# Attention into two mixture-of-experts layers: loads, halves of mixed tiles and the logits of layer 1's last block put elsewhere

## The chip, the cores and the metric

The kernel runs on one core of a Trainium2 chip. The metric is device time in microseconds of one launch; lower is better. Engines: TensorE (PE; PEld is its weight load), VectorE (DVE), ScalarE (ACT), GpSimd (POOL), and SyncE (SP), which only issues loads and stores. Every engine executes its own instructions strictly in the order of the program, so a wait at one instruction holds everything behind it on that engine.

## The reference

```python
# attention: 8 batches, 8 heads, 576 queries, head_dim 64; k and v averaged over runs of 8 rows
k_p = k.reshape(B, H, Sp, pool, D).mean(axis=3)
v_p = v.reshape(B, H, Sp, pool, D).mean(axis=3)
scores = scale * np.matmul(q, k_p.transpose(0, 1, 3, 2))
attn = softmax(scores);  x = attn @ v_p          # 4608 tokens of 512
# layer 1: 8 experts, top 1
logits = x @ w_gate + modality_bias[modality_id]
e_idx = np.argmax(logits, axis=1)
x = gate_w[:, None] * (relu(x @ w1[e_idx]) @ w2[e_idx])
# layer 2: the same with a skip score, and the input added
do_compute = x @ w_skip > 0
out = x.copy()
out[do_compute] += gate_w * (relu(x @ w1[e]) @ w2[e])     # experts by argmax(x @ w_gate)
```

## The kernel before, in words

**Attention.** The 4608 query rows are 36 columns of 128, nine for each pair of batches. A unit of q is a half-batch of 256 rows (two columns, one load of 512 KB into `q_sb`); the last 64 rows of both batches of a pair make up a merged column (numbers 8, 17, 26, 35), whose halves belong to different batches (`parts(c)`). Keys and values come in as raw tiles (`kb` or `kt`, and `v`), are summed over runs of 8 rows by VectorE (line 176) or GpSimd (lines 181 to 183), turned by TensorE (`prep_kb`, line 203 on) and stand as `KB` and `VB`. For column c, ScalarE spreads q (`split_q`, line 167), TensorE turns it (line 280), ScalarE copies it (`qt`, line 284), `emit_S` (line 296) makes scores against `KB`, VectorE takes the maximum `mx` (line 307), TensorE subtracts it (line 327), ScalarE takes exp (331), TensorE turns the result (348), and `emit_AV` (line 355) multiplies by `VB`. `emit_S` and `emit_AV` loop over `parts(c)` outside and over head pairs inside, so a merged column has all instructions of its first half, then all of its second. Each fp32 matmul appears twice in the trace: 8 and 12 instructions in a regular column, 16 and 24 in a merged one.

The order around the loads is written by hand: the prologue (lines 482 to 495) issues the first loads on SyncE's queue, and `wg`, `midi`, `bb` (router weights, modality ids, bias) on ScalarE's; the loop over c (line 560 on) issues q with `next_q`, keys and values with `next_kv`; `pool_at` (line 424) says at which c which sums are taken; VectorE's work of a column is put behind the `mx` of the next. 24 transposes of the identity keep TensorE at work while the first load is on its way (lines 512 to 514).

**Layer 1** works in blocks of 256 sorted tokens (halves t = 0, 1): gathered rows are turned into `xh` and `xl`, `gemm1` (line 1402) has 8 steps f, each followed by `hh` (ACT, 1406) and `hl` (DVE, 1407); `gemm2` (line 1455) has 8 steps per half. The blocks' outputs are layer 2's inputs: for each half 9 sums on VectorE (8 logits and the skip score, line 1734, `logit`) are queued in `todo` together with `first` and `second`, the two parts of layer 2's routing of that block (`picks`, lines 1660 to 1722: chains of small GpSimd and VectorE steps that end in the scatter of the rows). `drip(n)` takes steps of cost n off that queue, at the f's that `body1` (line 1895) sets by hand. Blocks 0 to 17 always run; 17 is `late`: it also loads what follows. Behind it a dynamic `If` runs further blocks where the routing needs them; with this input the trace has one more, 18 (`end` is set in its body). Behind that `first2` (line 1593) makes layer 2's first block: its `gemm1` steps alternate with what is left of block 18's logits, and `late_logits` (line 1576) makes the second half's 9 on TensorE instead: 4 transposes, a copy, 4 small matmuls. Then come `first` (f = 2), `second` and the last gather of layer 2's input (f = 4), whose rows the first `gemm2` turns.

Of the kernel before, what the change touches and what calls it, by code (L numbers as in the profile page):

```python
# [9 lines left out]
F32 = mybir.dt.float32  # L10
# [45 lines left out]
def attention(tc, g, q, k, v, mid, w_gate, bias, const, moe):  # L56
# [4 lines left out]
    with ExitStack() as ctx:  # L61
# [140 lines left out]

        def prep_kb(b, eng=None):
# [5 lines left out]
            for i in range(4):  # L209
                nc.tensor.transpose(ps[0:64, 126 * i:126 * i + 126], ks[0:126, i, :],  # L210
                                    g.ident[0:126, 0:126])
                nc.tensor.matmul(ps[64:128, 126 * i:126 * i + 126], lhsT=ks[0:126, i, :],
                                 rhs=g.ident[0:126, 0:126], start=True, stop=True)

            nc.tensor.matmul(ps[64:128, 0:SP], lhsT=ks[0:SP, 4, :], rhs=g.ident[0:SP, 0:SP],
                             start=True, stop=True)
            view = lambda c: ps[:, c:c + 6 * SP].rearrange("p (a s) -> p a s", s=2 * SP)[:, :, 0:SP]
# [78 lines left out]
        def emit_S(c, then=lambda: None):  # L296
            t = qT.pop(c)
            ps = ps_s.tile([128, 2, 512], F32, tag="s", name="ps_s")
            for b, p0, p1 in parts(c):
                for hp in range(4):  # L300
# [56 lines left out]
        def emit_AV(c):  # L357
# [7 lines left out]
            for b, p0, p1 in parts(c):  # L365
                for j in range(6):
                    o = (j % 3) * VW
# [49 lines left out]
        def idle():  # L417
            for _ in range(3):
# [5 lines left out]
        pool_at = {0: [(pool_kb, 1, 2, 4, P)],  # L424
                   1: [(pool_kb, 1, 0, 2, V), (pool_kb, 1, 4, 5, V), (pool_v, 1, 0, P)]}
# [64 lines left out]
        for i in range(2):  # L490
            nc.scalar.dma_start(out=wg[64 * i:64 * i + 64],
                                in_=w_gate.rearrange("(h d) e -> d h e", d=64))
        nc.scalar.dma_start(out=midi,
                            in_=mid.bitcast(I32).rearrange("(b s w) -> b s w", s=S, w=2))
        nc.scalar.dma_start(out=bb, in_=bias.unsqueeze(0).to_broadcast([128, 2, E]))
# [14 lines left out]
        P.memset(WGV, 0.0)  # L510

        ps = ps_q.tile([128, 4, 128], F32, tag="q", name="ps_w")
        for i in range(24):
            nc.tensor.transpose(ps[:, i % 4, :], g.ident, g.ident)
# [44 lines left out]
        for c in range(NC + LAG):  # L559
            if c < NC:  # L560
                next_q(cols[c][0] + 4)
                next_kv(c)
                next_q(cols[c][0] + 5)
# [607 lines left out]
class Moe:  # L1171
# [404 lines left out]
    def late_logits(self, i):  # L1576

        nc = self.nc
        ps = self.ps_t("ps_x2")
        for k in range(4):  # L1580
            nc.tensor.transpose(ps[:, k, :], self.x2[i % 2][:, 1, 128 * k:128 * k + 128],
                                self.g.ident)
        xt = self.o2[1].rearrange("p (k n) -> p k n", k=4)
        nc.scalar.copy(xt, ps)
        yield
        lg = self.pp.tile([128, E + 1], F32, tag="m", name="ps_lg")
        for k in range(4):
            nc.tensor.matmul(lg, lhsT=xt[:, k, :], rhs=self.g.w9c[:, k, :], start=(k == 0),
                             stop=(k == 3))
        nc.vector.tensor_copy(self.lg2[i % 2][:, 1, :], lg)  # L1590
        yield

    def first2(self, n):
# [4 lines left out]
        todo = [x for x in self.todo[:-11]]  # L1598
# [4 lines left out]
        for f in range(8):  # L1603
            self.gemm1(n, f)
            for x in todo[2 * f:2 * f + 2 if f < 7 else None]:
                x[2]()
            if f in (0, 2):
                next(late)
# [150 lines left out]
class Layer:  # L1759
# [129 lines left out]
    def body1(self, i, end):  # L1889
# [35 lines left out]
        if more:  # L1925
            m.load_split(i + 1)
            if end is None:
                m.gates1(i + 1, m.sp)
            m.split_w1_if(range(4))
        at = {f: m.drip for f in ((0, 1, 3, 5) if late else (0, 1, 5, 6) if i > 8 else  # L1930
                                  (0, 1, 3, 5, 6))}
# [3 lines left out]
        if more and late:  # L1935
            m.drip(3)
            next_x(0)
            next_x(1)
            m.split_w1_if(range(4, 8))
            m.drip(4)  # L1940
        else:
            if more:
                m.split_w1_if(range(4, 8))
            m.drip(7)
        with m.tc.If(full > 0):
# [127 lines left out]
```

## Time and profile before

| what | value |
|---|---|
| median of 3 runs | 964.8 us (963.85 to 965.71) |
| the profiled execution's own time | 967.72 us |
| its span in the trace | 966.0 us |
| mean granted clock of TensorE in it | 0.966 |
| attention alone on TensorE, and mixed with layer 1's first blocks | to about 78 us, and to about 230 us |
| layer 1's block 17, `gemm2` | 643.8 to 656.8 us |
| block 18 | 658.0 to 682.6 us |
| layer 2's first block: `gemm1`, and its first `gemm2` | 682.5 to 700.3, and to 719.9 us |

A row of the timeline gives the start, the duration of a run of like instructions, the engine and line, what it writes and reads with shapes, and in brackets the idle time before it with what released it. The granted clock is a share of 2.4 GHz; 0.5 is the lower of its two levels, 1.2 GHz. Durations of TensorE overlap, since matmuls are pipelined.

### The profile page before, as it was taken

The numbers are of one execution on the slowest core, as the hardware profiler recorded it, in microseconds if no ns is written. First come the engines' busy times: TensorE is split into PE (matmuls) and PEld (weight loads), VectorE is DVE, ScalarE is ACT, GpSimd is POOL, SyncE is SP. The second block draws the span as 40 slices with busy tenths as digits, with TensorE's granted clock in tenths as the row PEclk, the third lists the DMA queues.
The fourth block names the chain that finished last, engine by engine and source line by source line (L and its number), as shares of the span: only waits on it lengthen the run. The fifth ranks groups of instructions, "written<-read, shape, count | busy, mean of one in ns | idle before, by whom it ended". The sixth has DMA issues, their size and how long they took to land. (4 is left out here: it accounts for less than half of the span.)

```text
span 966.0 us, 19093 instructions
## 1 busy us (share of the span) xinstructions
PE 908.6 (94%) x6205; PEld 813.6 (84%) x6205; DVE 696.9 (72%) x1844; ACT 373.2 (39%) x734; POOL 517.6 (54%) x762
## 2 busy tenths in 40 slices
PE   6899999899999999998999989999889999999995
PEld 5798898887899999996999878988868988978983
DVE  4376787765787878889877798877775667667555
ACT  2465566544122222242222332212413556565454
POOL 4744698304246547666656556575653344354443
PEclk7799999998999999998999999999999999999998
DMA  9997884521321211251223512127213774581341
GB/s 224 216 257 212 231 232 148 156 102 53 119 71 57 79 60 64 92 200 64 74 78 100 205 54 86 65 68 241 77 45 129 219 218 148 177 259 35 110 155 41
DMA packets 87225, 126.03 MB, mean 130 GB/s; under 512 B 14328, under 2 KB 51192, under 8 KB 86954
## 3 DMA queue, kind: packets, MB, share of 16 engines
q1 hardware_dynamic: 75386, 96.68, 32.9%
q0 software_dynamic: 10480, 27.59, 9.3%
q8 instruction: 62, 1.02, 0.4%
q14 instruction: 81, 0.66, 0.2%
q10 hardware_dynamic: 1216, 0.08, 0.1%
HBM read 184.18 MB, written 39.50 MB: 232 GB/s over the span
## 5 line engine op out<-in xcount | busy, mean ns | idle before, releaser
L1402 PE MATMUL ps_g<-xh,w1h 128*128 128x256 f32 x896 | 256.8, 287 | 5.7 <-DVE hl L1407 3.1
L1402 PE MATMUL ps_g<-xl,w1h 128*128 128x256 f32 x896 | 254.1, 284 | 2.6 <-DVE xl L1354 2.6
L1402 PE MATMUL ps_g<-xh,w1l 128*128 128x256 f32 x896 | 253.7, 283 | 0.0
L1734 DVE CUSTOM_DVE_ANT_0 junk<-x,W 128x512 bf16<-128x512 f32 x333 | 234.8, 705 | 19.6 <-DVEq L1332 6.6
L1455 PE MATMUL ps_g<-w2h,hh 128*128 128x512 f32 x464 | 192.9, 416 | 0.7 <-DVE rs_v L1043 0.5
L1455 PE MATMUL ps_g<-w2h,hl 128*128 128x512 f32 x464 | 186.7, 402 | 6.6 <-DVE hl L1407 6.6
L1455 PE MATMUL ps_g<-w2l,hh 128*128 128x512 f32 x464 | 186.3, 402 | 0.0
L1402 PEld LDWEIGHTS ps_g<-xh,w1h 128*128 128x128 f32 x896 | 170.6, 190 | 12.0 <-DVE hl L1407 3.5
L1402 PEld LDWEIGHTS ps_g<-xl,w1h 128*128 128x128 f32 x896 | 169.9, 190 | 4.5 <-DVE xl L1354 3.6
L1402 PEld LDWEIGHTS ps_g<-xh,w1l 128*128 128x128 f32 x896 | 169.9, 190 | 0.0
L1406 ACT ACTIVATE hh<-ps_g 128x512 fp32r<-128x512 f32 (+1 forms) x116 | 67.7, 584 | 250.8 <-PE ps_g L1402 235.2
L906 POOL TENSOR_SCALAR OB<-iota,BB,pay 128x128 bf16<-128x128 bf16 x126 | 112.2, 898 | 22.7 <-DVE BB L894 20.3
L1407 DVE SCALAR_TENSOR_TENSOR hl<-ps_g,hh 128x512 fp32r<-128x512 f32 (+1 forms) x116 | 77.5, 668 | 61.5 <-ACT hh L1406 37.7
L1455 PEld LDWEIGHTS ps_g<-w2h,hl 128*128 128x128 f32 x464 | 89.1, 192 | 30.8 <-DVE hl L1407 8.2
L1455 PEld LDWEIGHTS ps_g<-w2h,hh 128*128 128x128 f32 x464 | 89.3, 192 | 19.8 <-ACT hh L1424 1.5
L1455 PEld LDWEIGHTS ps_g<-w2l,hh 128*128 128x128 f32 x464 | 89.4, 193 | 16.9
L1322 POOL TENSOR_TENSOR w1l<-w1r,w1h 128x512 fp32r<-128x512 f32 x39 | 50.6, 1316 | 64.4 <-ACT w1h L1321 64.2
L1344 DVE TENSOR_TENSOR w2l<-w2r,w2h 128x512 fp32r<-128x512 f32 x112 | 75.2, 708 | 7.9 <-ACT w2h L1343 5.4
L1700 POOL DMA_INDIRECT out_dram<-x,dsi x38 | 46.7, 1228 | 46.7 <-ACTq L1337 10.6
L1321 ACT CAST w1h<-w1r 128x512 fp32r<-128x512 f32 x120 | 68.3, 620 | 0.5 <-ACT hh L1406 0.5
L1343 ACT CAST w2h<-w2r 128x512 fp32r<-128x512 f32 x112 | 63.9, 616 | 4.0 <-DVE gidxf L1046 2.5
L368 PE MATMUL ps_av<-VB,et 96*128 96x146 f32 (+1 forms) x480 | 64.5, 288 | 0.0
(292 smaller groups left out, 1384.7 us busy)
## 6 DMA issues: line engine op xcount, KB each, us to landing
w1r<-in_moe_w_dram SPq DMA_DIRECT2D x128, 512.0 KB
w2r<-in_moe_w_dram SPq DMA_DIRECT2D x128, 512.0 KB
x2s<-x SPq DMA_DIRECT2D x19, 522.0 KB
v<-in_v_dram SPq DMA_DIRECT2D x48, 192.0 KB
xd<-x SPq DMA_DIRECT2D x16, 520.0 KB
q_sb<-in_q_dram SPq DMA_DIRECT2D x16, 512.0 KB
kt<-in_k_dram SPq DMA_DIRECT2D x32, 144.0 KB
x2s<-OBx SPq DMA_DIRECT2D x16, 261.0 KB
```

Of the source, the lines that this page charges most:

```text
L368: nc.tensor.matmul(ps[p0:p1, j // 3, o:o + 2 * VW], lhsT=t[:, j, p0:p1], rhs=VB[b % NR][:, j].rearrange("p i w -> p (i w)"), start=(j % 3 ...
L906: e.tensor_scalar(g.ob(c)[:, i, :], g.iota, r.BB[:, c:c + 1], r.pay[:, i, c:c + 1], ALU.is_equal, ALU.mult)
L1321: self.nc.scalar.copy(self.w1h[f], raw)
L1322: (eng or self.nc.vector).tensor_tensor(self.w1l[f], raw, self.w1h[f].bitcast(F32), ALU.subtract)
L1343: self.nc.scalar.copy(self.w2h[f], raw)
L1344: (eng or self.nc.vector).tensor_tensor(self.w2l[f], raw, self.w2h[f].bitcast(F32), ALU.subtract)
L1402: nc.tensor.matmul(out, lhsT=a[f][:, k, :], rhs=b[:, k, :], start=(n == 0), stop=(n == 11))
L1406: nc.scalar.activation(out=hh, in_=whole, func=ACTF.Relu)
L1407: nc.vector.scalar_tensor_tensor(hl, in0=whole, scalar=0.0, in1=hh.bitcast(F32), op0=ALU.max, op1=ALU.subtract)
L1455: nc.tensor.matmul(ps, lhsT=a[f][:, tt], rhs=b[f], start=(n == 0), stop=(n == 23))
L1700: self.nc.gpsimd.indirect_dma_start(out=self.out, out_offset=bass.IndirectOffsetOnAxis(ap=self.dsi[i % 2][:, t:t + 1], axis=0), in_=self.x ...
L1734: self.nc.vector.tensor_tensor_reduce(out=self.junk, in0=self.x2[i % 2][:, t, 0:DM], in1=self.W9[:, e, :], scale=1.0, scalar=0.0, op0=ALU. ...
```

## The change

It has five parts. (1) At the start, `midi`, `bb` and the two `wg` loads go from ScalarE's queue to GpSimd's, behind its last memset; 12 more transposes of the identity stand in the middle of the first `prep_kb` and 10 behind it. (2) The two VectorE sums of batch 1's keys go from c = 1 to c = 0; at c = 2 the load of half-batch 5 is put ahead of that step's v load. (3) `emit_S` and `emit_AV` take the halves of a merged column in turn. (4) In block 17, `second` of block 16 is taken out of the queue, three sums are taken and both halves of block 18's rows are turned ahead of it; in the dynamic blocks behind, the queue is drained evenly from f = 0 to 7, and the last half-block's 9 sums (t = 0) are left to the block behind. (5) `first2` makes both halves' 9 logits on TensorE (f = 0, 1, 2) and has no sums on VectorE.

```diff
             d = sums_of(("v", b), [VC, 6, D])
             pool_rows(d[:, 3 * hf + i0:3 * hf + i1, :], raw_t["v", b, hf][:, i0:i1, :], eng)
 
+        def keep_busy(n):
+            ps = ps_q.tile([128, 4, 128], F32, tag="q", name="ps_w")
+            for i in range(n):
+                nc.tensor.transpose(ps[:, i % 4, :], g.ident, g.ident)
+
         def prep_kb(b, eng=None):
 
             bg.settle()
...
             ps = ps_m.tile([128, 512], F32, tag="m", name="ps_k")
             KBb = KB[b % NR]
             for i in range(4):
+                if b == 0 and i == 2:
+                    keep_busy(12)
                 nc.tensor.transpose(ps[0:64, 126 * i:126 * i + 126], ks[0:126, i, :],
                                     g.ident[0:126, 0:126])
                 nc.tensor.matmul(ps[64:128, 126 * i:126 * i + 126], lhsT=ks[0:126, i, :],
...
 
             nc.tensor.matmul(ps[64:128, 0:SP], lhsT=ks[0:SP, 4, :], rhs=g.ident[0:SP, 0:SP],
                              start=True, stop=True)
+            if b == 0:
+                keep_busy(10)
             view = lambda c: ps[:, c:c + 6 * SP].rearrange("p (a s) -> p a s", s=2 * SP)[:, :, 0:SP]
             copy = nc.vector.tensor_copy if eng is nc.vector else nc.scalar.copy
             copy(KBb[0:64, 0:3, 0:SP], view(0)[0:64])
...
         def emit_S(c, then=lambda: None):
             t = qT.pop(c)
             ps = ps_s.tile([128, 2, 512], F32, tag="s", name="ps_s")
-            for b, p0, p1 in parts(c):
-                for hp in range(4):
+            for hp in range(4):
+                for b, p0, p1 in parts(c):
                     nc.tensor.matmul(ps[p0:p1, hp // 2, (hp % 2) * 144:(hp % 2) * 144 + 144],
                                      lhsT=t[:, hp, p0:p1], rhs=KB[b % NR][:, hp, :],
                                      start=(hp % 2 == 0), stop=(hp % 2 == 1),
...
                 ps = ps_e.tile([128, 2, 512], F32, tag="et", name="ps_av")
             else:
                 ps = ps_a.tile([128, 2, 512], F32, tag="av", name="ps_av")
-            for b, p0, p1 in parts(c):
-                for j in range(6):
-                    o = (j % 3) * VW
+            for j in range(6):
+                o = (j % 3) * VW
+                for b, p0, p1 in parts(c):
                     nc.tensor.matmul(ps[p0:p1, j // 3, o:o + 2 * VW],
                                      lhsT=t[:, j, p0:p1],
                                      rhs=VB[b % NR][:, j].rearrange("p i w -> p (i w)"),
...
         av_t = {}
 
         P, V = nc.gpsimd, nc.vector
-        pool_at = {0: [(pool_kb, 1, 2, 4, P)],
-                   1: [(pool_kb, 1, 0, 2, V), (pool_kb, 1, 4, 5, V), (pool_v, 1, 0, P)]}
+        pool_at = {0: [(pool_kb, 1, 2, 4, P), (pool_kb, 1, 0, 2, V), (pool_kb, 1, 4, 5, V)],
+                   1: [(pool_v, 1, 0, P)]}
         for t, c0 in enumerate((3, 8, 16, 23)):
             pool_at[c0] = [(pool_k, t, 0, P)]
             pool_at[c0 + 1] = [(pool_k, t, 1, P)]
...
         next_kv(0, 5)
         next_q(3)
         next_kv(0, 1)
-        for i in range(2):
-            nc.scalar.dma_start(out=wg[64 * i:64 * i + 64],
-                                in_=w_gate.rearrange("(h d) e -> d h e", d=64))
-        nc.scalar.dma_start(out=midi,
-                            in_=mid.bitcast(I32).rearrange("(b s w) -> b s w", s=S, w=2))
-        nc.scalar.dma_start(out=bb, in_=bias.unsqueeze(0).to_broadcast([128, 2, E]))
 
         for i in range(NR):
             me = nc.vector if i < 1 else nc.gpsimd
...
         for i in range(NR):
             P.tensor_copy(VB[i][:, :, :, D], half)
         P.memset(WGV, 0.0)
-
-        ps = ps_q.tile([128, 4, 128], F32, tag="q", name="ps_w")
-        for i in range(24):
-            nc.tensor.transpose(ps[:, i % 4, :], g.ident, g.ident)
+        P.dma_start(out=midi, in_=mid.bitcast(I32).rearrange("(b s w) -> b s w", s=S, w=2))
+        P.dma_start(out=bb, in_=bias.unsqueeze(0).to_broadcast([128, 2, E]))
+        for i in range(2):
+            P.dma_start(out=wg[64 * i:64 * i + 64],
+                        in_=w_gate.rearrange("(h d) e -> d h e", d=64))
+
+        keep_busy(24)
 
         midf = one.tile([128, C1], F32, name="midf")
         mid8 = xp.tile([128, 2, XW], F32, tag="x", name="mid8")
...
         route_at = {12: (0, 9), 21: (9, 9), 30: (18, 9)}
         for c in range(NC + LAG):
             if c < NC:
-                next_q(cols[c][0] + 4)
+                next_q(cols[c][0] + (5 if c == 2 else 4))
                 next_kv(c)
                 next_q(cols[c][0] + 5)
             if c in (22, 32, 36):
...
     def late_logits(self, i):
 
         nc = self.nc
-        ps = self.ps_t("ps_x2")
-        for k in range(4):
-            nc.tensor.transpose(ps[:, k, :], self.x2[i % 2][:, 1, 128 * k:128 * k + 128],
-                                self.g.ident)
-        xt = self.o2[1].rearrange("p (k n) -> p k n", k=4)
-        nc.scalar.copy(xt, ps)
-        yield
-        lg = self.pp.tile([128, E + 1], F32, tag="m", name="ps_lg")
-        for k in range(4):
-            nc.tensor.matmul(lg, lhsT=xt[:, k, :], rhs=self.g.w9c[:, k, :], start=(k == 0),
-                             stop=(k == 3))
-        nc.vector.tensor_copy(self.lg2[i % 2][:, 1, :], lg)
+        xt = [o.rearrange("p (k n) -> p k n", k=4) for o in self.o2]
+        for t in range(2):
+            ps = self.ps_t("ps_x2")
+            for k in range(4):
+                nc.tensor.transpose(ps[:, k, :], self.x2[i % 2][:, t, 128 * k:128 * k + 128],
+                                    self.g.ident)
+            nc.scalar.copy(xt[t], ps)
+            yield
+        lg = self.pp.tile([128, 2, E + 1], F32, tag="m", name="ps_lg")
+        for t in range(2):
+            for k in range(4):
+                nc.tensor.matmul(lg[:, t, :], lhsT=xt[t][:, k, :], rhs=self.g.w9c[:, k, :],
+                                 start=(k == 0), stop=(k == 3))
+        nc.vector.tensor_copy(self.lg2[i % 2], lg)
         yield
 
     def first2(self, n):
...
         nc, g = self.nc, self.g
         ranks = self.ranks
         self.ranks = []
-        todo = [x for x in self.todo[:-11]]
+        for _, cost, f in self.todo[:-2]:
+            if not cost:
+                f()
         first, second, third = self.picks(n - 1, False)
         self.todo = []
         nc.vector.tensor_copy(self.gate0, self.gate[n % 2])
         late = self.late_logits(n - 1)
         for f in range(8):
             self.gemm1(n, f)
-            for x in todo[2 * f:2 * f + 2 if f < 7 else None]:
-                x[2]()
-            if f in (0, 2):
+            if f < 3:
                 next(late)
             if f == 1 and n % 2:
                 nc.scalar.copy(self.xg[0], self.xg[1])
...
             if end is None:
                 m.gates1(i + 1, m.sp)
             m.split_w1_if(range(4))
-        at = {f: m.drip for f in ((0, 1, 3, 5) if late else (0, 1, 5, 6) if i > 8 else
-                                  (0, 1, 3, 5, 6))}
+        if end is None:
+            at = {f: m.drip for f in ((0, 1, 5, 6) if i > 8 else (0, 1, 3, 5, 6))}
+        elif late:
+            at = {f: m.drip for f in (0, 1, 3, 5)}
+        else:
+            n = sum(x[1] for x in m.todo) - 2
+            at = {f: partial(m.drip, (n + j) // 5) for j, f in enumerate((0, 1, 3, 5, 6))}
+            at[7] = m.drip
         if more and not late:
             at.update({2: lambda: next_x(0), 4: lambda: next_x(1)})
         m.gemm2(i, 0, self.epilogue, at)
-        if more and late:
+        if late:
+            _, _, second = m.todo.pop(0)
             m.drip(3)
             next_x(0)
             next_x(1)
+            second()
+        if more:
             m.split_w1_if(range(4, 8))
-            m.drip(4)
-        else:
-            if more:
-                m.split_w1_if(range(4, 8))
+        if end is None:
             m.drip(7)
+        elif not late:
+            m.drip()
         with m.tc.If(full > 0):
             m.gemm2(i, 1, self.epilogue)
 
```

## Rows read from the trace of the kernel before

**Rows 1.** The page: busy time, share of the span and instructions of each engine.
```profile
PE 908.6 (94%) x6205; PEld 813.6 (84%) x6205; DVE 696.9 (72%) x1844; ACT 373.2 (39%) x734; POOL 517.6 (54%) x762
```

**Rows 2.** Stretches: busy us (instructions) of PE, PEld, DVE, ACT, POOL; granted clock; DMA share; GB/s.
```profile
0.00:20.00 20.00, 11.48 (x49) 9.17 (x50) 6.36 (x9) 4.15 (x6) 6.14 (x24) 0.75 0.90 221
20.00:44.00 24.00, 19.81 (x100) 16.18 (x100) 10.20 (x9) 10.32 (x27) 18.06 (x17) 0.64 0.99 217
44.00:78.00 34.00, 32.06 (x270) 31.05 (x270) 25.41 (x58) 21.76 (x48) 19.82 (x37) 1.00 0.91 237
```

**Rows 3.** Timeline, 0 to 22: start, duration, engine, line, operation, [idle before <- releaser].
```profile
13.10 0.57 ACTq L493 DMA_DIRECT2D midi<-in_moe_modality_id_dram  x1
...
15.92 0.62 ACT L167 COPY qs<-q_sb 128x512 f32<-128x512 f32 x1 [13.62 <-DMA v<-in_v_dram]
...
18.38 2.29 PE L301 MATMUL ps_s<-KB,qt 128*128 128x144 f32 x8 [0.68 <-ACT qt L284]
```

**Rows 4.** Timeline, 28 to 60: batch 1's keys turned, and the fourth column's scores.
```profile
34.28 0.39 PE L210 MATMUL ps_k<-ident,kb 126*64 126x126 f32 x1 [2.48 <-DVE kb L176]
...
40.38 2.27 PE L301 MATMUL ps_s<-KB,qt 128*128 128x144 f32 x8
```

**Rows 5.** Timeline, TensorE 100 to 112 and 204 to 214: scores and values, regular and merged.
```profile
101.89 1.15 PE L301 MATMUL ps_s<-KB,qt 128*128 128x144 f32 x8
...
106.01 1.74 PE L301 MATMUL ps_s<-KB,qt 128*64 128x144 f32 x16
...
110.03 0.51 PE L327 MATMUL ps_s<-mx,nident 128*128 128x288 f32 x2 [1.04 <-DVE mx L307]
...
206.54 1.66 PE L368 MATMUL ps_av<-VB,et 96*128 96x146 f32 x12
...
210.68 2.77 PE L368 MATMUL ps_av<-VB,et 96*64 96x146 f32 x24
```

**Rows 6.** Timeline, 42 to 63: loads of half-batches 5 and 6, and the copy of 6.
```profile
42.83 0.39 SPq L141 DMA_DIRECT2D q_sb<-in_q_dram  x1
...
55.59 0.39 SPq L141 DMA_DIRECT2D q_sb<-in_q_dram  x1
...
62.45 1.05 ACT L167 COPY qs<-q_sb 128x1024 f32<-128x1024 f32 x1
```

**Rows 7.** Timeline, 650 to 662: the seam between blocks 17 and 18 of layer 1.
```profile
654.88 0.17 DVE L1681 TENSOR_REDUCE rt_my<-rt_eq 128x2 f32<-128x16 f32 x1 [4.79 <-POOL rt_eq L1675]
...
656.91 0.20 POOL L1686 TENSOR_TENSOR carry<-carry,M 128x8 f32<-128x8 f32 x1
...
657.99 0.39 PE L1402 MATMUL ps_g<-xh,w1h 128*128 128x256 f32 x1 [1.18 <-ACTq L1332]
...
658.83 0.39 PE L1402 MATMUL ps_g<-xl,w1h 128*128 128x256 f32 x1 [0.45 <-DVE xl L1354]
```

**Rows 8.** VectorE's groups, 683 to 703: line, operation, count | busy us, mean ns | idle.
```profile
L1734 DVE CUSTOM_DVE_ANT_0 junk<-x,W 128x512 bf16<-128x512 f32 x9 | 6.2, 691 | 0.2
```

**Rows 9.** Timeline, 683 to 709: layer 2's first block behind block 18.
```profile
683.92 0.66 PE L1581 MATMUL ps_x<-ident,x 128*128 128x128 f32 x4
...
686.58 0.67 POOL L1686 TENSOR_TENSOR carry<-carry,M 128x8 f32<-128x8 f32 x1
...
687.26 0.95 PE L1588 MATMUL ps_lg<-w9c,o 128*128 128x9 f32 x8
...
691.93 0.99 POOL L1700 DMA_INDIRECT out_dram<-x,dsi  x1 [2.28 <-ACT w2h L1343]
...
695.48 0.39 PE L1402 MATMUL ps_g<-xh,w1h 128*128 128x256 f32 x1 [2.88 <-DVE hl L1407]
...
695.62 0.74 POOL L1665 COPY x<-lg 128x18 f32<-128x18 f32 x1 [2.70 <-DVE lg L1590]
...
708.27 0.66 PE L1350 MATMUL ps_x<-ident,xg 128*128 128x128 f32 x4 [1.89 <-DMA xg<-x2s,gidxf]
```

**Rows 10.** The stretch behind the first of those gaps, columns as in rows 2.
```profile
695.90:699.40 3.50, 3.50 (x20) 3.41 (x19) 2.20 (x4) 0.00 (x0) 2.92 (x10) 0.51 0.41 153
```

## The prediction, made before the changed kernel ran

> **What bounds the kernel now.** I began with the page's busy times: TensorE works in 94% of the span, VectorE in 72%, and no other engine in more than 54% [rows 1]. A gain is therefore TensorE idle time, TensorE time at the lower clock, or fewer matmul slots; what the change saves on other engines counts only where TensorE waits for it. Next I read the busy times by stretch, to see where TensorE's 57 idle microseconds lie. The first 44 us hold 8.5 + 4.2 = 12.7 of them, with a mean clock of 0.75 and 0.64 and a DMA share of 0.90 and 0.99. From 44 to 78 the clock is full and TensorE busy in 32.1 of 34, but DMA is still at 0.91 [rows 2]. So the start is short of data, not of TensorE. Last I read the timeline at three places that the diff names: the start, a merged column, and the seams around block 18.
>
> **Start, parts 1 and 2.** ScalarE's issue of `midi` sits at 13.10, its copy of the first q at 15.92, and TensorE's first scores follow only at 18.38 [rows 3]. The issue takes 0.57, and `bb` and two `wg` issues stand on the same queue. Put on GpSimd's queue they no longer stand ahead of the copy; the cost is four issues on a GpSimd that has nothing else until it has keys to sum. Its own sums for c = 0 are queued behind them, and if an issue is held there as `midi`'s was until 13.10, they start later; they are wanted only at 34.28 [rows 4], and that is their cover. The 22 added transposes run in the 8.5 us in which TensorE is idle before 20 [rows 2]; if q came at once they would cost their own time, by the mean of the instructions there (11.48 for 49, 0.23) some 5 us. The two sums moved to c = 0 attack the 2.48 us that TensorE waits at 34.28 for `kb`; where the mean clock is 0.64 [rows 2], the fourth column's scores take 2.27, at 40.38, against 1.15 in a later regular column [rows 4, 5]. So columns 0 to 3 could come 5 to 11 us earlier (2.8 for the copy from 15.92 back to 13.10 and 2.48, and a part of the time lost at half clock, in which a mean of 0.75 over 20 us and of 0.64 over 24 says that TensorE spent 10 + 17 = 27 us).
>
> How much of that lasts? Half-batch 5 is issued at 42.83 and half-batch 6 at 55.59; the copy of 6 runs at 62.45, 6.9 us behind its issue [rows 6], and DMA has no room to bring it sooner, with a share of 0.91 up to 78. So of 5 to 11 us of lead the most is eaten at these two copies. Half-batch 5 alone goes ahead in the queue, and the v load and the keys that it passes come that much later; behind a wait of ScalarE's copy for q stand its exp and its copies for the columns before, and TensorE waits for those. Bounds: -2 (the passed loads of one v and kt become the late ones, about the 2.48 of the wait above) and +8 (all of the lead lasts). I take **+1.5**, near the low end, since the copy at 62.45 comes within 7 us of its issue and the copy's successors have to follow it.
>
> **Halves in turn, part 3.** A merged column's scores take 1.74 and its values 2.77, a regular one's 1.15 and 1.66 [rows 5]. The number of instructions is doubled (16 for 8, 24 for 12), each on 64 of the 128 output partitions; if the two halves ran fully side by side, the extra 0.59 + 1.11 = 1.70 would go, at four merged columns 6.8. If two neighbours already overlap all they can, or the order brings nothing, it is 0. A loss I exclude: the same instructions run, and the longest they could take is one behind the other, in which each of the added 20 costs the 0.07 to 0.09 that these differences already show. Scores are followed by a maximum on VectorE for which TensorE waits 1.04 in the next column [rows 5]; where it does, the 0.59 is given back. At columns 17 and 35 I find the same and leave out three such terms of 0.59: 6.8 - 1.8 = **5.0**.
>
> **The last blocks, parts 4 and 5.** VectorE's `rt_my` at 654.88 waits 4.79 for GpSimd's `rt_eq`, with the turn of block 18's rows (`xl`) queued behind; TensorE waits 1.18 and 0.45 [rows 7]. With the turn ahead of `second` both go: 1.63. The four `split_w1_if` steps behind `second` come later, but the first is wanted four gemm1 steps on.
>
> In `first2` VectorE does nine sums of 691 ns, 6.2 us [rows 8], in two parts around a branch, and `hl` is late behind them: TensorE waits 2.88 at 695.48 [rows 9]. Those nine go. GpSimd then starts on the last picks at 695.62, having waited 2.70 for VectorE's copy of the logits, and the chain ends with the rows of the next block, for which TensorE waits 1.89 at 708.27. With no sums ahead of it the copy comes right behind step f = 2, about 5 us earlier, more than the 1.89. So 2.88 + 1.89 = 4.77.
>
> Added on TensorE: four transposes, 0.66, and eight small matmuls, 0.95 [rows 9], so 1.61. ScalarE's one copy more hides in its idle time, at 39% busy [rows 1]; without it, it would cost about the 0.62 of a copy of that size [rows 3]. In block 18, nine sums of the first half move from its own tail into the same place, `first2`, and vanish there. Handoff: 1.63 + 4.77 - 1.61 = **4.8**. Upper bound: behind the gap of 2.88 the clock is at 0.51 for 3.5 us [rows 10], so half of those, 1.7, is lost; without the gap that may be full, and a second such stretch follows the later wait: 4.8 + 3.4 = 8.2. Lower bound 0: the two waits stay, and 1.63 pays for the additions.
>
> Of the GpSimd steps in this chain the same one, `carry`, takes 0.20 when VectorE waits and 0.67 while sums run beside it [rows 7, 9]. The Trainium skill, page "SBUF — State Buffer", section "Who interferes with whom", says why such a pair may clash: a VectorE instruction with two SBUF operands and a GpSimd one share a port, and the one that starts later is blocked in full. These two rows agree. By that rule the seven small steps of that kind would each be 0.47 shorter once the sums are gone, an estimate of up to 3.3 us more from the handoff, and the total below would be 950 instead of 953.5.
>
> **Sum.** 1.5 + 5.0 + 4.8 = 11.3. The profiled execution took 967.7, so 956.4; it stood 2.9 above the median of 964.8, so **953.5**.
>
> **The rivals.**
> - *The loads bind less than I think* (12%): the lead of the start lasts, 8 in place of 1.5, so 947. For it: half-batch 5 comes sooner, and the 5 to 11 us are real idle time. Against it: DMA share of 0.91 to 78.
> - *The last picks do not move* (18%): in block 18 `first` stands at f = 7 and `second` behind four weight splits. GpSimd's picks of block 17 then end no sooner, as now with its scatter issue at 691.93 [rows 9], and those of 18 begin right behind that. The 1.89 stays, so the handoff gives 4.8 - 1.9 = 2.9 or less, 1.5 if half of the 2.88 stays as well. By the latter 1.5 + 5.0 + 1.5 = 8.0, and 967.7 - 8.0 - 2.9 = 957.
> - *The halves run as before* (8%): the chip takes matmuls to different halves one after the other in either order. Then 6.3 in all, 958.5.
> - *Slower* (4%): the lead lets TensorE run dry at half-batches 5 and 6, between 44 and 78, where it is at full clock now [rows 2]. A dry spell is where the clock fell to its lower level, 1.2 GHz, elsewhere [rows 9, 10], and a column at half clock costs more by 2.27 - 1.15 = 1.1 for its scores [rows 4, 5], 1.66 for its values, if these double too, and some 0.1 for the small rest: 2.9. Three such columns eat most of the gain of 11.3; from the fourth on (11.6) the kernel is slower. With five, 14.5, it ends at 953.5 + 14.5 = 968. Against it: five columns are 20 us of dry loads, and TensorE is busy in 94% of that stretch today.
>
> **How the numbers follow.** The forecast holds 58%, and its own bounds of -2 to +8, 0 to 6.8 and 0 to 8.2 seldom fall together: 949 to 958. The range of **946.5 to 960.5** takes in the first three rivals. The measurement of this kernel tells about 0.2% (2 us) from no change. Slower by more than that is the last rival, 0.04; the same, where that rival and the gains balance, 0.03; faster, all else, 0.93.
>
> **What would show it.** *Start*: scores of column 0 near 14, the wait at `prep_kb(1)` gone, but the copy of half-batch 6 at 61 or later, preceded by a wait on its load. *Halves*: merged scores near 1.2 and values near 1.7. *Last blocks*: no wait of VectorE's `rt_my` ahead of `xl` at the seam; no sum of line 1734 in `first2`; the picks' first copy 5 us nearer to the start of its gemm1; no wait at the first turn of the next rows. The forecast is wrong if columns 9 and on come 5 us or more earlier than 1.5 explains, if merged rows keep their durations, or if the stretch from 78 us on, which the change touches at only four merged columns and one seam, moves by more than 10 us.

## The result, and the profile after

The changed kernel took 954.6 us (median of 4 runs, 954.5 to 955.4) against 964.9 of the kernel before: ratio 0.9896, 95% interval 0.9879 to 0.9913. Measured again beside other kernels it took 954.3 against 963.0: 0.9907 (0.9890 to 0.9923). So it is faster by 8.7 to 10.2 us; the forecast was 11.3 less, 953.5, in a range of 946.5 to 960.5.

The page after, busy time by engine, against [rows 1]:

```profile
PE 897.7 (94%) x6239; PEld 803.9 (84%) x6239; DVE 689.6 (72%) x1826; ACT 373.4 (39%) x735; POOL 518.7 (54%) x766
```

TensorE has 34 instructions more and is busy 11 us less: the gain is mostly time at the higher clock and matmuls that overlap, and its idle time went only from 57 to 55 us.

The first three stretches, in the columns of [rows 2]:

```profile
0.00:20.00 20.00, 16.54 (x107) 13.91 (x108) 11.10 (x13) 8.09 (x20) 11.07 (x29) 1.00 0.92 225
20.00:44.00 24.00, 19.10 (x117) 15.70 (x115) 8.25 (x15) 10.31 (x22) 17.11 (x17) 0.79 0.95 223
44.00:78.00 34.00, 30.24 (x244) 28.66 (x245) 25.35 (x56) 18.82 (x41) 21.73 (x38) 0.95 0.98 258
```

The clock rose from 0.75 to 1.00 and from 0.64 to 0.79, but the third stretch lost: TensorE is busy in 30.2 of 34, before in 32.1. But a window of fixed bounds holds other work in the two kernels, so the timeline decides, against [rows 3, 4, 6] (start, duration, engine, line, operation, idle before and its releaser):

```profile
6.24 0.81 POOL L514 DMA_DIRECT2D midi<-in_moe_modality_id_dram  x1
...
9.59 0.62 ACT L167 COPY qs<-q_sb 128x512 f32<-128x512 f32 x1 [7.29 <-DMA q_sb<-in_q_dram]
...
13.74 1.25 PE L310 MATMUL ps_s<-KB,qt 128*128 128x144 f32 x8 [0.68 <-ACT qt L293]
...
23.49 1.02 DVE L176 TENSOR_REDUCE kb<-kb 72x64 f32<-72x512 f32 x1 [1.95 <-DMA kb<-in_k_dram]
...
25.23 0.51 PE L336 MATMUL ps_s<-mx,nident 128*128 128x288 f32 x2 [1.93 <-DVE mx L316]
...
28.02 0.42 PE L217 MATMUL ps_k<-ident,kb 126*64 126x126 f32 x1
...
54.77 0.39 SPq L141 DMA_DIRECT2D q_sb<-in_q_dram  x1
...
59.27 1.04 ACT L167 COPY qs<-q_sb 128x1024 f32<-128x1024 f32 x1 [3.22 <-DMA q_sb<-in_q_dram]
...
61.68 0.44 PE L255 MATMUL ps_v<-ident,v 96*128 96x96 f32 x3 [0.94 <-POOL VB L260]
...
63.49 1.84 PE L310 MATMUL ps_s<-KB,qt 128*128 128x144 f32 x8 [1.36 <-ACT ec L340]
```

The first scores come 4.6 us earlier and the wait for batch 1's keys at `prep_kb` is gone. It has only moved: the sums taken earlier now stand ahead of column 2's maximum on VectorE, the last of them waits 1.95 for its keys, and TensorE waits 1.93 for that maximum, where before it waited 0.20 (at 30.85). By the starts of the maxima the lead is 7.5 us at column 1 (18.80 against 26.31), 5.6 at column 2 and 6.2 at column 3, so it comes from the first q and not from these sums.

Half-batch 6 is issued at 54.77, only 0.8 earlier, so ScalarE's copy now waits 3.22 for it, where before it waited for nothing. Behind the copy ScalarE's exp is late, and TensorE waits 1.36 for it (the 0.94 ahead of that is a wait for GpSimd's `VB`); after that the next scores take 1.84 in place of 1.15, and the stretch's mean clock is 0.95.

Merged columns, against [rows 5]:

```profile
100.36 1.20 PE L310 MATMUL ps_s<-KB,qt 128*64 128x144 f32 x16
...
104.38 0.51 PE L336 MATMUL ps_s<-mx,nident 128*128 128x288 f32 x2 [1.58 <-DVE mx L316]
...
204.79 1.72 PE L377 MATMUL ps_av<-VB,et 96*64 96x146 f32 x24
```

Scores went from 1.74 to 1.20, values from 2.77 to 1.72: a merged column costs nearly what a regular one does (1.15 and 1.66). At this column, 17, the wait for the maximum grew from 1.04 to 1.58 and ate the scores' 0.54.

The seam of blocks 17 and 18, against [rows 7]:

```profile
643.20 1.29 DVE L1360 TENSOR_TENSOR xl<-ps_x,xh 128x512 fp32r<-128x512 f32 x2 [0.76 <-ACT xh L1359]
...
644.68 0.16 DVE L1689 TENSOR_REDUCE rt_my<-rt_eq 128x2 f32<-128x16 f32 x1
...
645.53 0.28 PE L1408 MATMUL ps_g<-xh,w1h 128*128 128x256 f32 x1
```

`xl` stands ahead of `rt_my`; TensorE no longer waits there, nor does `rt_my`, and `xl` waits 0.76 for ScalarE. Layer 2's first block, against [rows 9]; its `gemm1` starts at 669.2, before at 682.5:

```profile
674.71 0.20 POOL L1694 TENSOR_TENSOR carry<-carry,M 128x8 f32<-128x8 f32 x1
...
676.38 1.10 POOL L1708 DMA_INDIRECT out_dram<-x,dsi  x1 [0.68 <-issue]
...
677.09 0.16 DVE L1598 COPY lg<-ps_lg 128x18 f32<-128x18 f32 x1
...
680.96 0.98 POOL L1708 DMA_INDIRECT out_dram<-x,dsi  x1 [3.48 <-DVE w2l L1350]
...
681.93 0.21 POOL L1673 COPY x<-lg 128x18 f32<-128x18 f32 x1
...
689.32 1.58 POOL L1320 DMA_INDIRECT xg<-x2s,gidxf  x1 [1.88 <-DMA out_dram<-x,dsi]
...
693.30 1.12 PE L1356 MATMUL ps_x<-ident,xg 128*128 128x128 f32 x4 [1.91 <-DMA xg<-x2s,gidxf]
```

The wait of 2.88 for `hl` is gone. The logits are there at 677.3, but GpSimd begins the picks at 681.93, since the pending scatter is issued first, and the wait of 1.9 for the next rows stays. The clock is at half around it. It fell ahead of that wait: TensorE had waited 1.11 and 1.23 for GpSimd's picks (matmuls at 686.10 and 687.49), and the mean clock from 686 to 690 is 0.83.

```profile
690.00:694.00 4.00, 1.66 (x7) 0.85 (x7) 1.04 (x5) 0.00 (x0) 3.02 (x4) 0.50 0.47 132
694.00:698.00 4.00, 4.00 (x13) 3.27 (x13) 1.97 (x6) 0.67 (x2) 4.00 (x7) 0.50 0.18 67
```

Where the time came from, by the start of the same work in the two profiled executions:

| work | before | after | lead |
|---|---|---|---|
| column 8, maximum | 64.84 | 57.81 | 7.0 |
| column 9 | 69.08 | 65.37 | 3.7 |
| column 11 | 80.61 | 76.53 | 4.1 |
| column 35 | 198.64 | 192.76 | 5.9 |
| layer 1, block 10 `gemm1` | 460.69 | 450.63 | 10.1 |
| block 17, `gemm2` | 643.84 | 633.46 | 10.4 |
| block 18, `gemm1` | 657.99 | 645.53 | 12.5 |
| layer 2's first block, `gemm1` | 682.46 | 669.19 | 13.3 |
| its `gemm2` | 700.10 | 683.44 | 16.7 |
| the next `gemm1` | 719.76 | 705.77 | 14.0 |

Of this the 4.2 between column 35 and block 10 come almost wholly from work that was not changed: only column 35's values, 1.05 shorter, lie in it. Two stretches there ran with a mean clock of 0.82 in the execution before and 1.00 in the one after, which makes 3.5; first the two of before, then the same work after:

```profile
219.50:238.00 18.50, 17.29 (x120) 13.75 (x119) 11.60 (x46) 8.11 (x10) 9.78 (x13) 0.82 0.10 30
442.00:461.00 19.00, 15.87 (x62) 12.08 (x62) 16.86 (x51) 2.60 (x6) 11.74 (x25) 0.82 0.24 80
```

```profile
213.30:230.30 17.00, 14.79 (x120) 11.84 (x119) 11.92 (x46) 8.11 (x10) 9.68 (x13) 1.00 0.12 33
434.00:451.00 17.00, 13.48 (x66) 10.58 (x66) 15.01 (x44) 2.65 (x6) 10.03 (x21) 1.00 0.26 89
```

From column 35's maximum to block 10 the execution before took 262.1; in the thirteen other traces, the changed kernel's two among them, the same work took 257.8 to 259.1. That is why the two spans lie 13.1 apart and the medians 8.7 to 10.2; the profiled execution of before stood 2.9 above its median.

### The profile page after: what moved, and what is told of

Its sections match the earlier page's. It is cut to its first block, busy times and chain, and to the rows that moved or that the text cites. A ratio compares the mean times of both kernels' runs of the same rounds, so it can differ in the third digit from the quotient of the medians.

```text
span 952.9 us, 19141 instructions
## 1 busy us (share of the span) xinstructions
PE 897.7 (94%) x6239; PEld 803.9 (84%) x6239; DVE 689.6 (72%) x1826; ACT 373.4 (39%) x735; POOL 518.7 (54%) x766
## 5 line engine op out<-in xcount | busy, mean ns | idle before, releaser
L1742 DVE CUSTOM_DVE_ANT_0 junk<-x,W 128x512 bf16<-128x512 f32 x324 | 228.2, 704 | 18.7 <-DVEq L1338 6.3
L1320 POOL DMA_INDIRECT xg<-xd,gidx x38 | 45.1, 1188 | 32.8 <-DVE rs_lo L1171 15.7
```

The source lines that it names most:

```text
L1320: self.nc.gpsimd.indirect_dma_start(out=self.xg[i % 2][:, t, 0:w], out_offset=None, in_=src, in_offset=bass.IndirectOffsetOnAxis(ap=gidx[: ...
L1742: self.nc.vector.tensor_tensor_reduce(out=self.junk, in0=self.x2[i % 2][:, t, 0:DM], in1=self.W9[:, e, :], scale=1.0, scalar=0.0, op0=ALU. ...
```

## The experiments

The theory was that all three groups of parts bring what the lead table shows beside the clock: start 4, halves 4, last blocks 3.6. The rivals were that what a part gains is waited for later. Ratios are to the kernel before on the same chip; one hundredth of a per cent is 0.1 us.

**Halves one after the other again.**

```diff
-            for hp in range(4):
-                for b, p0, p1 in parts(c):
+            for b, p0, p1 in parts(c):
+                for hp in range(4):
...
-            for j in range(6):
-                o = (j % 3) * VW
-                for b, p0, p1 in parts(c):
+            for b, p0, p1 in parts(c):
+                for j in range(6):
+                    o = (j % 3) * VW
```

> The changed kernel with part 3 undone: both halves of a merged column one after the other again. Theory: each merged column takes its old time, and that lasts to the end: 1.6 + 1.1 + 1.1 + 0.5 = 4.2 us more than the changed kernel, some 958.9. Rival: the columns after a merged one wait for VectorE's maxima, which took back 1.2 at column 24 and 1.0 at column 27 of the changed kernel's trace; then it is 2.0 more, 956.7. If nothing of part 3 lasts, 954.6.

958.2, ratio 0.9948 (0.9929 to 0.9967): 3.9 to 5.0 us of the gain go. The spans are the old ones, and so is the wait for the maximum:

```profile
104.12 1.74 PE L310 MATMUL ps_s<-KB,qt 128*64 128x144 f32 x16
...
108.11 0.51 PE L336 MATMUL ps_s<-mx,nident 128*128 128x288 f32 x2 [1.01 <-DVE mx L316]
```

**Part 3 alone on the kernel before.**

```diff
-            for b, p0, p1 in parts(c):
-                for hp in range(4):
+            for hp in range(4):
+                for b, p0, p1 in parts(c):
...
-            for b, p0, p1 in parts(c):
-                for j in range(6):
-                    o = (j % 3) * VW
+            for j in range(6):
+                o = (j % 3) * VW
+                for b, p0, p1 in parts(c):
```

> The kernel before with part 3 alone: halves in turn. Theory: a merged column's scores take 1.2 and its values 1.7, as in the changed kernel, and 3.5 to 5 us of it last: 4.2 below the kernel before. Rival: later waits for loads and for VectorE's maxima take back more than half, as columns 11 to 35 of the changed kernel's traces have it (1.3 to 2.9 net): 2 below.

958.0, ratio 0.9951 (0.9930 to 0.9971): 4.7 us. Adding part 3 alone and taking it alone away agree, and the rival of 2 lies below the interval here (2.8 to 6.7) and at the edge of it there. It holds in part inside the trace: in the changed kernel, at column 24, `rt_my` of the routing waits 1.89 for GpSimd, and TensorE 1.18 for the maximum behind it.

```profile
133.68 0.23 DVE L851 TENSOR_REDUCE rt_my<-rt_eq 128x9 f32<-128x72 f32 x1 [1.89 <-POOL rt_eq L845]
...
135.98 0.51 PE L336 MATMUL ps_s<-mx,nident 128*128 128x288 f32 x2 [1.18 <-DVE mx L316]
```

**Last blocks as before**: `late_logits`, `first2` and the end of `body1` as in the kernel before (parts 4 and 5 undone), of which these lines decide:

```diff
-        for _, cost, f in self.todo[:-2]:
-            if not cost:
-                f()
+        todo = [x for x in self.todo[:-11]]
...
+            for x in todo[2 * f:2 * f + 2 if f < 7 else None]:
+                x[2]()
...
-        if late:
-            _, _, second = m.todo.pop(0)
+        if more and late:
             m.drip(3)
             next_x(0)
             next_x(1)
-            second()
...
```

> The changed kernel with parts 4 and 5 undone: the last blocks of layer 1 and layer 2's first block as before. Theory: the lead grew from 10.3 us at block 17's second matmuls to 13.9 behind layer 2's first block, so 3.6 are lost: 958.2. Prediction's term: 4.8, 959.4. Rival: GpSimd's last picks start no earlier in either kernel, and only the 1.6 of the seam and part of the 2.9 are real, the rest a stretch of low clock: 956.5.

958.0, ratio 0.9952 (0.9931 to 0.9972): 4.3 to 5.4 us, uncertain by some 2.5. Its trace shows less of that in its place: from block 17's second matmuls to the `gemm1` behind layer 2's first block it takes 73.4, the two traces of the changed kernel 72.3 and 71.0, the kernel before 75.9. The old wait for `hl` is back:

```profile
684.76 0.39 PE L1408 MATMUL ps_g<-xh,w1h 128*128 128x256 f32 x1 [2.08 <-DVE hl L1413]
```

**Part 4 undone, part 5 kept**; the sums that block 18's tail then makes on VectorE are made again on TensorE.

```diff
...
-        else:
-            n = sum(x[1] for x in m.todo) - 2
-            at = {f: partial(m.drip, (n + j) // 5) for j, f in enumerate((0, 1, 3, 5, 6))}
-            at[7] = m.drip
+        at = {f: m.drip for f in ((0, 1, 3, 5) if late else (0, 1, 5, 6) if i > 8 else
+                                  (0, 1, 3, 5, 6))}
...
-        if late:
-            _, _, second = m.todo.pop(0)
+        if more and late:
             m.drip(3)
             next_x(0)
             next_x(1)
-            second()
-        if more:
             m.split_w1_if(range(4, 8))
-        if end is None:
+            m.drip(4)
+        else:
+            if more:
+                m.split_w1_if(range(4, 8))
             m.drip(7)
-        elif not late:
-            m.drip()
```

> The changed kernel with part 4 undone and part 5 kept: blocks 17 and 18 as before, layer 2's first block with both halves' logits on TensorE. Theory: the waits of 1.2 and 0.5 at the seam of blocks 17 and 18 return, and seven sums stand again behind block 18's second matmuls, so hl is late in layer 2's first block: 3 to 4 us more than the changed kernel. Rival: part 5 alone brings most, 1.6 more.

956.9, ratio 0.9938 (0.9916 to 0.9961): 3.0 us more than the changed kernel, with intervals that overlap. In the trace the seam's waits return, and from block 17's second matmuls to layer 2's first it takes 37.4 us, in the changed kernel beside it 35.8: 1.6 more, the rival's figure. The times do not tell 1.6 from 3.0. No wait for `hl` returned, so that half of the theory fell: that wait belonged to the sums inside `first2`, part 5.

```profile
645.18 0.38 PE L1408 MATMUL ps_g<-xh,w1h 128*128 128x256 f32 x1 [0.70 <-ACTq L1338]
...
646.02 0.39 PE L1408 MATMUL ps_g<-xl,w1h 128*128 128x256 f32 x1 [0.45 <-DVE xl L1360]
```

**Start as before** (parts 1 and 2 undone; the loads stand on ScalarE's queue again).

```diff
...
-        pool_at = {0: [(pool_kb, 1, 2, 4, P), (pool_kb, 1, 0, 2, V), (pool_kb, 1, 4, 5, V)],
-                   1: [(pool_v, 1, 0, P)]}
+        pool_at = {0: [(pool_kb, 1, 2, 4, P)],
+                   1: [(pool_kb, 1, 0, 2, V), (pool_kb, 1, 4, 5, V), (pool_v, 1, 0, P)]}
...
+        nc.scalar.dma_start(out=midi,
+                            in_=mid.bitcast(I32).rearrange("(b s w) -> b s w", s=S, w=2))
...
-        P.dma_start(out=midi, in_=mid.bitcast(I32).rearrange("(b s w) -> b s w", s=S, w=2))
...
-                next_q(cols[c][0] + (5 if c == 2 else 4))
+                next_q(cols[c][0] + 4)
```

> The changed kernel with parts 1 and 2 undone: loads on ScalarE's queue, no added transposes, the old order of sums and loads. Theory: the lead of 4.0 us at column 11 lasts, so 958.7, and the maxima of columns 0 to 3 come 5 to 7 us later. Prediction's term: 1.5, 956.1. Rival: the lead of 7.0 at column 8 is the true one and later stalls are the same in both, so 961.

955.2, ratio 0.9923 (0.9897 to 0.9950): 1.5 to 2.6 us, inside the uncertainty of either comparison (some 3 us), so the times alone do not exclude the theory's 4; the column times speak against it. Column 11 came at 78.5, and in three other kernels with the new start at 77.9, 79.3 and 80.4: the lead at column 8 is lost by column 11, and 44 to 78 is as full with the old start as in the kernel before:

```profile
44.00:78.00 34.00, 32.05 (x275) 31.04 (x274) 26.05 (x62) 21.18 (x48) 19.89 (x37) 1.00 0.86 233
```

**Without the added transposes.**

```diff
-                if b == 0 and i == 2:
-                    keep_busy(12)
...
-            if b == 0:
-                keep_busy(10)
```

> The changed kernel without the 22 added transposes at the start. Theory: they hold the clock at full in the first 20 us (granted 1.00 there, 0.75 before), so without them it falls to half, and columns 0 to 2 come some 2 us later; but half-batch 6 lands at the same time, so from column 9 on nothing changes: within 1 us of the changed kernel at the end. Rival: the lead of the start counts in full, 2 to 4 us more.

954.5, ratio 0.9910 (0.9895 to 0.9925): nothing. The clock is still at 0.91 in the first 20 us without them, against 0.75 in the kernel before, so most of its rise comes from what is left of the new start. The theory that columns 0 to 2 come later fell: column 0's maximum came at 13.9, earlier than the 15.0 with them, since q's transposes stand behind the last ten of them.

```profile
0.00:20.00 20.00, 15.65 (x89) 12.90 (x89) 11.83 (x13) 8.86 (x22) 12.06 (x30) 0.91 0.94 239
```

**The changed kernel again**, with no edit (the repeat).

> The changed kernel itself, so that the others of this call can be compared with it on the same chip. In its first measurement it was 10.2 below the kernel before. If 4 of those are the lead at column 11, which the runs of the first call had at 1 to 3 only, the difference here is nearer 7 us; if that lead was no accident, 10.

954.3, ratio 0.9907 (0.9890 to 0.9923); column 11 at 78.3, and ScalarE waits 5.8 for half-batch 6. The lead of 4 at column 11 was an accident of the two executions compared: the kernel before was there at 80.6, part 3 alone, with the same old start, at 77.3.

**The gather ahead of the picks, the scatter behind them** (`free` is the list of what waited in the queue at no cost, here that scatter).

```diff
-        for _, cost, f in self.todo[:-2]:
-            if not cost:
-                f()
+        free = [f for _, cost, f in self.todo[:-2] if not cost]
...
             if f == 2:
+                self.gather(g.r2.gidx0, 2, 1, g.x2s[0:16 * T, :])
                 first()
...
                 second()
-                self.gather(g.r2.gidx0, 2, 1, g.x2s[0:16 * T, :])
+                for x in free:
+                    x()
                 third()
```

> The changed kernel with one step moved: in layer 2's first block the gather of the next block's rows is issued at f = 2 ahead of the last picks, and the pending scatter of block 17's second half goes behind the picks. Theory: GpSimd holds the picks behind that scatter (issued 680.96, picks from 681.93, logits there since 677.3) and the rows behind the picks; both come earlier, the wait of 1.91 for the rows goes, that of 1.1 and 1.2 in the rank matmuls shrinks, and with them the stretch at half clock: 3 to 6 us less, 949 to 951.5. Rival: the routing that follows the picks sets the end of that stretch, and it gives back what is gained: 954.6.

955.7, ratio 0.9922 (0.9892 to 0.9952): no gain, and the theory of 3 to 6 fell. The wait for the rows is gone, but the rank matmul waits 1.96 for the picks, which stand behind two gathers.

```profile
680.63 1.10 POOL L1708 DMA_INDIRECT out_dram<-x,dsi  x1 [0.68 <-ACT w2h L1349]
...
685.14 1.24 POOL L1320 DMA_INDIRECT xg<-x2s,gidxf  x1 [3.41 <-ACT w2h L1349]
...
692.07 0.17 PE L1721 MATMUL R<-M,trim 128*128 128x16 bf16 x1 [1.96 <-POOL M L1692]
```

The issue behind the first scatter comes 4.5 us after it, as the second scatter did in the changed kernel (676.38 to 680.96), though it is another transfer; what fills that time the profile does not show.

**Only the scatter behind the picks** (`free` as above).

```diff
...
                 second()
                 self.gather(g.r2.gidx0, 2, 1, g.x2s[0:16 * T, :])
+                for x in free:
+                    x()
                 third()
```

> The changed kernel with one issue moved: in layer 2's first block the pending scatter of block 17's second half goes behind the last picks and the gather. Theory: GpSimd's issue behind the branch, at 680.96 in the changed kernel, holds the picks, whose logits are there at 677.3; without it they start about 4 us earlier against the block's first matmul (8.5 in place of 12.7), the waits of 1.1 and 1.2 in front of the rank matmuls and of 1.9 for the gathered rows go, and with them a stretch at half clock: 3 to 6 us less than the changed kernel. Rival: the picks start earlier, but the routing behind them or a clock that falls all the same sets the end of that block: within 1 us of it.

953.9, ratio 0.9900 (0.9880 to 0.9920): within 1 us of the changed kernel beside it, as the rival had it; the 3 to 6 of the theory did not come. The picks' first copy comes 9.2 us behind the block's first matmul (671.6), near the 8.5 expected, in place of 12.7, and the waits in front of the rank matmuls are gone. The wait for the rows is not: GpSimd's second part of the picks stands at f = 4 and the gather behind it. The rows come 2.8 earlier against the block's first matmul (21.3 in place of 24.1), but TensorE gets there as much earlier.

```profile
680.79 0.19 POOL L1673 COPY x<-lg 128x18 f32<-128x18 f32 x1 [1.74 <-issue]
...
689.12 1.51 POOL L1320 DMA_INDIRECT xg<-x2s,gidxf  x1 [1.95 <-ACT w2h L1349]
...
692.95 1.12 PE L1356 MATMUL ps_x<-ident,xg 128*128 128x128 f32 x4 [1.85 <-DMA xg<-x2s,gidxf]
```

**The gather between the two parts of the picks**, the scatter behind them (`free` as above).

```diff
...
                 first()
+                self.gather(g.r2.gidx0, 2, 1, g.x2s[0:16 * T, :])
...
                 second()
-                self.gather(g.r2.gidx0, 2, 1, g.x2s[0:16 * T, :])
+                for x in free:
+                    x()
                 third()
```

> The changed kernel with the gather of the next block's rows issued between the two parts of the last picks (f = 2), and block 17's pending scatter behind both. Theory: the gather is what TensorE waits 1.9 for, in the changed kernel and with the scatter late as well, since it stands behind the picks' second part; here it lands some 4 us earlier, the 1.9 goes, the ranks come up to 2 us later: 1 to 3 us less than the changed kernel. Rival: GpSimd's time per issue only moves the wait to the rank matmuls: within 1 us.

955.9, ratio 0.9911 (0.9886 to 0.9936): the rival, by the trace more than by the times, whose interval does not exclude 1 to 2 us. The rows come in time, and the rank matmul waits 3.76.

```profile
693.80 0.17 PE L1721 MATMUL R<-M,trim 128*128 128x16 bf16 x1 [3.76 <-POOL M L1692]
...
698.55 0.63 PE L1356 MATMUL ps_x<-ident,xg 128*128 128x128 f32 x4
```

So in all four orders this stretch waits for GpSimd's string of issues and picks, and another order moved the wait without a gain that the times show.

**Half-batch 6 ahead of its step's keys and values.**

```diff
-                next_q(cols[c][0] + (5 if c == 2 else 4))
+                next_q(cols[c][0] + (5 if c in (2, 4) else 4))
```

> The changed kernel with half-batch 6 also put ahead: at c = 4 its load is issued before that step's keys and values. Theory (the loads as a whole bind, not one load's place): the copy of half-batch 6 no longer waits (3.2 to 6.3 in the changed kernel's traces), but the keys and values that it passes land as much later and GpSimd's sums of them are late instead; column 11 within 1.5 of the changed kernel's 76.6 to 78.4, the end within 1.5 of it. Rival (only the place in the queue binds): the lead of some 7 us at column 8 lasts, column 11 comes near 74, and the kernel is 3 to 4 us faster than the changed one.

951.5, ratio 0.9874 (0.9848 to 0.9899). The load is issued at 50.70, the copy runs at 55.69 without a wait, and the lead of 7 at column 8 lasts: column 11 at 72.5, column 35 at 187.2 against 192.8 and 192.9 in the two traces of the changed kernel. That is the rival, and the theory that the loads as a whole bind there fell: TensorE is as busy from 44 to 78 as with the old start, at full clock, while the DMA share is 0.96.

```profile
50.70 0.39 SPq L141 DMA_DIRECT2D q_sb<-in_q_dram  x1
...
55.69 1.05 ACT L167 COPY qs<-q_sb 128x1024 f32<-128x1024 f32 x1
```

```profile
44.00:78.00 34.00, 32.05 (x285) 30.60 (x284) 27.65 (x62) 22.61 (x50) 21.66 (x38) 1.00 0.96 259
```

**Every half-batch ahead.**

```diff
-                next_q(cols[c][0] + (5 if c == 2 else 4))
+                next_q(cols[c][0] + (5 if c > 1 else 4))
```

> The changed kernel with every half-batch's load, from c = 2 on, issued ahead of its step's keys and values. With half-batch 6 alone ahead, the kernel was 2 to 3 us faster than the changed one, and ScalarE still waited 3.7 for two later loads of q, but TensorE only 1.95 for one maximum near 67. Theory (each half-batch's place in the queue bound in its turn): a further 1 to 2 us off, ratio to the kernel before near 0.985. Rival (the loads as a whole bind from there on): keys and values are late in its place, and it is at or above 0.987.

950.2, ratio 0.9875 (0.9849 to 0.9901): the same, so only half-batch 6's place bound. The ratio is the rival's, but not for its reason: keys and values are not late, TensorE's only wait from 40 to 82 is again 1.95 for a maximum. Both are the fastest kernels of the study, some 3 us below the changed one by their ratios (0.9875 to 0.9907); the intervals overlap a little, so the times alone do not settle that, and the column times are what speaks for it.

## Why the prediction was right, and where it was not

- **Sum.** Forecast 11.3 less; measured 8.7 to 10.2. Start 1.5, measured 1.5 to 2.6 (each of these differences is uncertain by some 3 us); halves 5.0, measured 4.7 alone and 3.9 to 5.0 undone; last blocks 4.8, measured 4.3 to 5.4.
- **Start.** The mechanism was right: a lead of 7 us at column 8, eaten by ScalarE's copy of half-batch 6. Its make-up was not: the first q's copy moved by 6.3 (15.92 to 9.59) in place of 2.8, and the 2.48 at `prep_kb` became a wait of 1.93 for column 2's maximum. The step "DMA has no room to bring it sooner, with a share of 0.91" failed. A busy share near one says that bytes are moving, not that these bytes could not move first: issued 4 us earlier, half-batch 6 arrived in time, and of what it passed nothing was late by as much (TensorE's longest wait from 40 to 82 is then 1.95, for a maximum). The rival "the loads bind less" needed one more load moved to come true. That the size came out as 1.5, picked between -2 and 8 for a reason that failed, is in part luck.
- **The added transposes** cost nothing at the end, and brought nothing; at column 0 they cost 1.1 (15.0 against 13.9).
- **Halves.** Right in mechanism and size, with the row that bounded it (the difference between a merged and a regular column). Of the three score terms left out, only column 17's was given back to the maximum; at columns 8, 26 and 35 some 0.5 each stayed in the repeat's trace. In their place stands the 1.2 lost at column 24, which the sum did not have. By the starts of the maxima, columns 11 to 35 take 117.5 without turns and 114.6 with them (the repeat); with the 0.5 at column 8 ahead of them that is 3.4, and column 35's values, 1.05 shorter, come behind.
- **Last blocks.** The seam's 1.63 and the 2.88 of `hl` went as forecast. The step "with no sums ahead of it the copy comes right behind step f = 2, about 5 us earlier, more than the 1.89" failed: the logits came early (677.1, 7.9 behind the block's first matmul, before 12.9), but GpSimd's first copy only went from 13.2 to 12.7, held by the scatter, and the 1.89 became 1.91. That is the rival "the last picks do not move" by another queue than it named. Nor was an earlier copy enough: with the scatter put behind the picks it came at 9.2, and the wait was still 1.85. Without the 1.89 the term is 2.9, which the measured 4.3 to 5.4, uncertain by 2.5, does not exclude. The lead table tells more: the seam and block 18 brought 2.9 (10.4 to 13.3; 1.6 by the trace with part 4 undone) in place of 1.63, and layer 2's first block only 0.7 (13.3 to 14.0), in the repeat 2.1, in place of the 3.2 that the rest of the term makes. That the whole came out near 4.8 is in part luck. Nor did the half-clock stretches of the upper bound go (3.5 and 3.4 us before): 690 to 698 is at 0.50.
- **GpSimd's steps.** `carry` takes 0.20 at 674.71, with no sums beside it, as by the rule of the Trainium skill ("SBUF — State Buffer", "Who interferes with whom"). The 3.3 us that this could have brought did not reach the end, since GpSimd then waited to issue.
- **Slower.** The price of the last rival did occur, at one or two columns (scores in 1.84 at 63.49), not at four.

## What to carry to other kernels

Where a stretch is short of data, ask of each late tile when its load was issued and what stood ahead of it in the queue, before reading a busy DMA as a bound. Where a chain is held by an engine that issues transfers, moving one issue moves the wait; count the issues between the data's arrival and the chain's first step. When single executions differ by stretches at a lower clock, compare starts of the same work, and read a difference in a stretch of unchanged work as chance.

## What the runs showed of the hardware that was not expected

- Matmuls on the two 64-column halves of the array overlap when they alternate: 16 take 1.20 in place of 1.74, and 24 take 1.72 in place of 2.77, the times of 8 and 12 on the full width (1.15 and 1.66).
- On GpSimd, an indirect DMA's issue behind another takes 1.8 to 1.9 us from start to start (685.14 and 686.90; 689.32 and 691.21), and the second one around a branch 4.5 to 4.6 (680.63 and 685.14; 676.38 and 680.96).
- Half-clock stretches come in some executions of unchanged work and not in others (0.82 against 1.00 in the two stretches near 220 and 450), and these two are worth 3.5 us of a span.
